# A retention stage ahead of two MLPs: loads behind the decay table, scores of a fifth chunk, and the order of the last rests

## The chip, the core and the metric

The kernel runs on one core of one Trainium2 chip, in one launch. The metric is the device time of an execution in microseconds; the kernel before takes 588.68 us (the median of three runs, 588.51 to 590.65).

## What is computed

Three blocks follow each other, all in float32. First a retention (a linear attention with decay): 2 batches, 8 heads, 768 positions, head size 64. Then an MLP with 512 inputs, 2048 hidden units and a leaky ReLU with a slope per unit, then a second MLP of the same sizes with a squared ReLU. The reference walks over blocks of 64 positions:

```
Dmask = where(i >= j, lam ** (i - j), 0)
intra = ((q_b @ k_b^T) * Dmask) @ v_b
inter = (q_b * lam ** (i + 1)) @ kv_state
out   = intra + inter
kv_state = lam ** block * kv_state + (k_b * lam ** (block - 1 - i))^T @ v_b

x = x @ w_in;  x = max(x, 0) + alpha * min(x, 0);  x = x @ w_out     # first MLP
x = x @ w_in;  x = max(x, 0) ** 2;                 x = x @ w_out     # second MLP
```

The result of the retention, 1536 tokens by 512 channels, is the input of the first MLP.

## The kernel before, in words

**The retention stage.** The kernel uses blocks of 128 positions, so there are 6 steps of 2 batches: 12 chunks, in the order step 0 of both batches, step 1 of both, and so on. Each chunk has four loads of 256 KB: keys `k` and queries `q` (`load_qk`, lines 298 and 299), values `v` and once more the keys, `r`, with positions first (`load_vk`, lines 306 and 310; the last two chunks have no `r`). For chunk n the steps are:

- `scores(n)`: 16 products q k into PSUM (line 422). Only two PSUM buffers exist for them. The scores of chunks 0 and 1 are copied to SBUF by ScalarE (line 427), because the decay table is not there yet; those of later chunks stay in PSUM until the decay.
- `decay(n)`: VectorE multiplies the scores by the decay table `dec` and writes SBUF (line 434).
- `factors(n)`: GpSimd scales `q` by the growth of the decay (line 441, chunks from 2 on) and `r` by the decay to the end of the block (line 444), in place.
- `outputs(n)`: TensorE computes scores times `v` (line 459), `q` times the state (line 467, chunks from 2 on) and the new state product `pk` (line 477).
- `keep_output(n)`: ScalarE rounds the output to the high half of the MLP's input, `xah` (line 486).
- `keep_state(n)`: VectorE adds `pk` to the old state (line 502), ScalarE scales the new one for its next use (line 508, four instructions).
- `keep_rest(n)`: the low half `xal`. For chunks 0 to 8, TensorE subtracts `xah` inside PSUM by a product with a negative unit matrix (`less`, line 495) and ScalarE copies the rest out (line 496). From chunk 9 on (`RESTS`), VectorE subtracts directly (line 493). The PSUM buffer of an output is free only after its rest; there are two, so `outputs(n)` waits for the rest of chunk n-2.

**The decay table.** It holds the powers of lam for all heads. VectorE computes the powers in a chain of small instructions with float32 corrections (lines 347 to 386) into a table `z` of 8 rows; it goes to DRAM (line 391) and comes back spread over 128 partitions as `dec` (line 393, 512 KB). Behind that load, `load_vk(1)` is gated: GpSimd first copies one element of `dec` into `v1` (line 305), so that SP issues no further load until the table has landed. Until then TensorE does the scores of chunks 0 to 3 (`FIRST` = 4), the growth table (line 402) and products with zeros (`keep_warm`, line 320): 12 at the very start and 10 after the scores (`WARM`). Each float32 product shows as two passes.

**Weights.** All MLP products are made in a split form: a float32 number is a rounded high half and a rest, and three products make one. Weights come in 64 pieces of 512 KB (`load_piece`, line 111), three raw buffers, and each is turned into a high and a low tile by a conversion unit: `start` (two ScalarE instructions, lines 122 and 123), `begin` (three VectorE instructions, lines 129 to 131), `middle` (one VectorE instruction, line 139, and ScalarE's rounding, line 141), `end` (one VectorE subtraction, line 150, which waits for the rounding). The first five units are done inside the retention stage, at the chunks marked in `EARLY_UNITS`; eight pieces are loaded at the chunks marked in `EARLY_LOADS`, on SP's queue. A later piece waits for a raw buffer, so for the unit three places before it.

**The order.** The schedule is manual: every engine and queue works through its instructions in program order. The loop over the chunks (lines 522 to 548) issues, for chunk n: the loads `q`, `k` of chunk n+4 and `v`, `r` of chunk n+2, a weight piece if marked; `outputs(n)`; `decay(n+2)`; `begin` of a unit if marked; `keep_output(n)`; `keep_state(n)`; `middle` and `end` of the unit; `start` of the next unit if the next chunk is marked; `factors(n+2)`; `scores(n+3)`; `keep_rest(n)`. After it come the MLPs (lines 561 to 584): 12 products of a hidden tile (line 172), activations, 12 products of the output (lines 225 and 227), with one unit a step.

Of the kernel before, what the change touches and what calls it, by code (L numbers as in the profile page):

```python
# [7 lines left out]
F32 = mybir.dt.float32  # L8
# [8 lines left out]
CH = 128  # L17
NCH = S // CH
NN = B * NCH
NPAIR = H // 2  # L20
# [5 lines left out]
CPT = TT // CH  # L26
ZW = 256
RESTS = 9
FIRST = 4
LA = 3  # L30
DA = 2
AHEAD = 3
# [8 lines left out]
ORDER = [(n // B, n % B) for n in range(NN)]  # L41

LEAST = 2.0**-15
WARM = 12, 10
EARLY_UNITS = [0, 0, 0, 1, 0, 1, 0, 1, 0, 1, 1, 0]
EARLY_LOADS = [0, 1, 1, 0, 1, 0, 1, 0, 1, 1, 1, 1]

SEQ = [0] + [p for f in range(1, 2 * NF) for p in (2 * f, 2 * f - 1)] + [4 * NF - 1]
SEQ[7:9] = SEQ[8:6:-1]
# [4 lines left out]
def retention_then_two_mlps(  # L54
# [15 lines left out]
    nc = tc.nc  # L70
# [83 lines left out]
    conv = Conversion()  # L154
# [114 lines left out]
    actx = ExitStack()  # L269
    ap1 = actx.enter_context(tc.tile_pool(name="ap1", bufs=1))  # L270
    ap2 = actx.enter_context(tc.tile_pool(name="ap2", bufs=2))
    qp = actx.enter_context(tc.tile_pool(name="qp", bufs=LA + 4))
    kp = actx.enter_context(tc.tile_pool(name="kp", bufs=LA + 2))
    scp = actx.enter_context(tc.tile_pool(name="scp", bufs=LA + 1))

    psc = actx.enter_context(tc.tile_pool(name="psc", bufs=2, space=PSUM))
    pso = actx.enter_context(tc.tile_pool(name="pso", bufs=2, space=PSUM))
# [23 lines left out]

    def load_vk(n):
        v_t = kp.tile([128, H, D], F32, tag="v", name=f"v{n}")
        if n == 1:
            nc.gpsimd.tensor_copy(v_t[:, 0, 0:1], dec[:, 0, 0:1])
        nc.sync.dma_start(v_t, vr[n])
        r_t = None
        if ORDER[n][0] < NCH - 1:
            r_t = kp.tile([128, H, D], F32, tag="r", name=f"r{n}")
            nc.sync.dma_start(r_t, kr[n])  # L310
        vk_t[n] = v_t, r_t
# [29 lines left out]
        nc.gpsimd.tensor_copy(head[:, :, t], m)  # L341

    keep_warm(0)
    for n in range(FIRST):
        load_qk(n)

    nc.vector.tensor_copy(sq[:, 0:1], lam_sb)
# [44 lines left out]
    load_vk(0)  # L392
    nc.sync.dma_start(dec, bass.AP(zd[:, :].tensor, zd[:, :].offset, [[1, 128], [ZW, H], [1, CH]]))
    dec_v = dec.rearrange("p (a t) i -> p t a i", t=2)

    grow = ap1.tile([128, NPAIR, CH], F32, name="grow")

# [18 lines left out]
    def scores(n):  # L416
        q_t, k_t = qk_t[n]
        ps = psc.tile([128, 2, NPAIR, CH], F32, tag="s", name=f"s{n}")
        for a in range(NPAIR):
            for t in range(2):  # L420
                rows = slice(t * D, (t + 1) * D)
                nc.tensor.matmul(  # L422
                    ps[:, t, a, :], k_t[rows, a, :], q_t[rows, a, :], start=True, stop=True
                )
        sc = scp.tile([128, 2, NPAIR, CH], F32, tag="sc", name=f"sc{n}")
        if n < FIRST - 2:
            nc.scalar.copy(sc, ps)
            ps = sc
        sc_t[n] = sc, ps

    def decay(n):
        sc, ps = sc_t[n]
        for a in [slice(0, 2), slice(2, 4)] if n == 0 else [slice(0, 4)]:
            nc.vector.tensor_tensor(sc[:, :, a], ps[:, :, a], dec_v[:, :, a], ALU.mult)  # L434

# [14 lines left out]
    def outputs(n):  # L450
        c, b = ORDER[n]
        q_t = qk_t.pop(n)[0]
        v_t, r_t = vk_t.pop(n)
        sc = sc_t.pop(n)[0]
        po = pso.tile([128, NPAIR, CH], F32, tag="o", name=f"o{n}")

        for a in range(NPAIR):
            for t in range(2):
                nc.tensor.matmul(  # L459
                    po[t * D : (t + 1) * D, a, :], v_t[:, 2 * a + t, :], sc[:, t, a, :],  # L460
                    start=a == 0, stop=c == 0, skip_group_check=True,
                )
        if c > 0:
            for a in range(NPAIR):
                for t in range(2):
                    d = slice(t * D, (t + 1) * D)
                    nc.tensor.matmul(  # L467
                        po[d, a, :], state[b, c % 2][d, a, :], q_t[d, a, :], start=False,
                        stop=True, skip_group_check=True,
                    )  # L470
        pk = None
        if c < NCH - 1:
            pk = psk.tile([128, 2, NPAIR, D], F32, tag="pk", name=f"pk{n}")[:, 0]
            for a in range(NPAIR):
                for t in range(2):
                    h = 2 * a + t
                    nc.tensor.matmul(  # L477
                        pk[t * D : (t + 1) * D, a, :], r_t[:, h, :], v_t[:, h, :], start=a == 0,
                        stop=True, skip_group_check=True,
                    )  # L480
        return po, pk
# [28 lines left out]
                )  # L510

    for n in range(FIRST):
        scores(n)
        if n == 2:
            growth()
    keep_warm(1)
    load_vk(1)
    for n in range(2):
        factors(n)
    for n in range(DA):  # L520
        decay(n)
    for n in range(NN):
        if n + FIRST < NN:
            load_qk(n + FIRST)
        if n + 2 < NN:
            load_vk(n + 2)
        if EARLY_LOADS[n]:
# [1 line left out]
        if n == 0:  # L529
            nc.sync.dma_start(alpha_sb, alpha)  # L530
        po, pk = outputs(n)
        if n + DA < NN:
            decay(n + DA)
        if EARLY_UNITS[n]:
            conv.begin()
        keep_output(n, po)
        if pk is not None:
            keep_state(n, pk)
        if EARLY_UNITS[n]:
            conv.middle(load=False)  # L540
            conv.end()
        if n + 1 < NN and EARLY_UNITS[n + 1] or n == NN - 1:
            conv.start(conv.k)
        if n + 2 < NN:
            factors(n + 2)
        if FIRST <= n + LA < NN:
            scores(n + LA)
        keep_rest(n, po)
    actx.close()
    psum["mlp"] = ctx.enter_context(  # L550
        tc.tile_pool(name="psum", bufs=1, space=PSUM, reuse_waits="tile")
# [93 lines left out]
```

## Time and profile before

| | |
|---|---|
| median of three runs | 588.68 us (588.51 to 590.65) |
| the profiled execution | 591.76 us |
| its span | 590.0 us |
| TensorE, products | 578.9 us busy (98%) |
| TensorE, weight loads | 479.9 us (81%) |
| VectorE | 360.1 us (61%) |
| ScalarE | 296.7 us (50%) |
| GpSimd | 28.3 us (5%), all in the first 57 us |

How to read it: the shares are means over the whole span, of which the retention stage is about the first 63 us. Most of the rest is the two MLPs, in which TensorE has no gaps worth a mention. An engine's share over the span therefore says little of the retention stage: GpSimd's 5% are half of its time there. The profiled execution is 3.08 us longer than the median of the unprofiled runs.

### The profile page before, as it was taken

The numbers are of one execution on the slowest core, as the hardware profiler recorded it, in microseconds if no ns is written. First come the engines' busy times: TensorE is split into PE (matmuls) and PEld (weight loads), VectorE is DVE, ScalarE is ACT, GpSimd is POOL, SyncE is SP. The second block draws the span as 40 slices with busy tenths as digits, with TensorE's granted clock in tenths as the row PEclk, the third lists the DMA queues.
The fourth block names the chain that finished last, engine by engine and source line by source line (L and its number), as shares of the span: only waits on it lengthen the run. The fifth ranks groups of instructions, "written<-read, shape, count | busy, mean of one in ns | idle before, by whom it ended". The sixth has DMA issues, their size and how long they took to land.

```text
span 590.0 us, 7970 instructions
## 1 busy us (share of the span) xinstructions
PE 578.9 (98%) x3069; PEld 479.9 (81%) x3069; DVE 360.1 (61%) x616; ACT 296.7 (50%) x515; POOL 28.3 (5%) x31
## 2 busy tenths in 40 slices
PE   8799899999999999999999999999999999999997
PEld 7688788888888888888888888888888888888885
DVE  4489897577578777887887787577522222222422
ACT  2476777566556766576576565555522222321220
POOL 1565000000000000000000000000000000000000
PEclk9799999999999999999999999999999999999999
DMA  6895334332436223233232132332100000400401
GB/s 215 284 390 187 107 112 142 139 108 96 167 130 213 77 103 108 96 118 108 106 111 104 41 139 74 141 107 73 73 0 1 0 1 0 143 0 1 142 1 72
DMA packets 25733, 62.39 MB, mean 106 GB/s; under 512 B 2904, under 2 KB 3936, under 8 KB 25696
## 3 DMA queue, kind: packets, MB, share of 16 engines
q1 hardware_dynamic: 17632, 32.53, 15.7%
q10 hardware_dynamic: 8064, 29.36, 14.5%
q8 instruction: 24, 0.39, 0.3%
q14 instruction: 13, 0.11, 0.1%
HBM read 52.44 MB, written 9.45 MB: 105 GB/s over the span
## 4 chain that ended last, share of the span: by engine, by line
PE 96%; DMA 2%; DVE 1%; issue 0%; DVEq 0%
PE h L172 44%; PE acc L227 22%; PE acc L225 22%; PE o L459 2%; PE o L467 2%; PE s L422 2%; PE pk L477 1%; DMA dec<-zd 1%; PE o L495 1%; DVE sc L434 0%; DMA zd<-z 0%; DMA lam_sb<-in_lam_dram 0%; DVE err L367 0%; DVE sq L349 0%; DVE ps L241 0%
## 5 line engine op out<-in xcount | busy, mean ns | idle before, releaser
L191 ACT CAST gh<-g 128x512 fp32r<-128x512 f32 x96 | 59.7, 621 | 92.6 <-DVE g L182 38.6
L182 DVE SCALAR_TENSOR_TENSOR g<-h,g 128x512 f32<-128x512 f32 x48 | 33.2, 691 | 117.3 <-ACT g L181 117.3
L181 ACT ACTIVATE g<-h 128x512 f32<-128x512 f32 x48 | 28.7, 597 | 124.9 <-PE h L172 124.9
L196 DVE TENSOR_TENSOR gl<-g,gh 128x512 fp32r<-128x512 f32 x96 | 66.5, 692 | 31.0 <-ACT gh L191 22.3
L172 PE MATMUL h<-xah,wl 128*128 128x512 f32 x192 | 74.8, 390 | 0.0
L172 PE MATMUL h<-xah,wh 128*128 128x512 f32 x192 | 74.7, 389 | 0.0
L172 PE MATMUL h<-xal,wh 128*128 128x512 f32 x192 | 74.7, 389 | 0.0
L225 PE MATMUL acc<-gh,wl 128*128 128x512 f32 x192 | 74.7, 389 | 0.0
L225 PE MATMUL acc<-gh,wh 128*128 128x512 f32 x192 | 74.7, 389 | 0.0
L225 PE MATMUL acc<-gl,wh 128*128 128x512 f32 x192 | 74.7, 389 | 0.0
L172 PE MATMUL h<-xbh,wl 128*128 128x512 f32 x192 | 74.7, 389 | 0.0
L172 PE MATMUL h<-xbl,wh 128*128 128x512 f32 x192 | 74.7, 389 | 0.0
L172 PE MATMUL h<-xbh,wh 128*128 128x512 f32 x192 | 74.7, 389 | 0.0
L227 PE MATMUL acc<-wl,gh 128*128 128x512 f32 x192 | 74.7, 389 | 0.0
L227 PE MATMUL acc<-wh,gh 128*128 128x512 f32 x192 | 74.7, 389 | 0.0
L227 PE MATMUL acc<-wh,gl 128*128 128x512 f32 x192 | 74.7, 389 | 0.0
L186 DVE SCALAR_TENSOR_TENSOR g<-h,g 128x512 f32<-128x512 f32 x42 | 29.0, 691 | 41.7 <-ACT g L185 41.6
L150 DVE TENSOR_TENSOR wl<-bits,wh 128x512 fp32r<-128x512 f32 x64 | 44.8, 699 | 3.9 <-ACT wh L141 3.8
L131 DVE SCALAR_TENSOR_TENSOR bits<-raw,bits 128x512 uint32<-128x512 uint32 x64 | 45.1, 704 | 2.2
L139 DVE CUSTOM_DVE_ANT_0 bits<-raw,bits 128x1024 uint16<-128x1024 uint16 x64 | 45.1, 705 | 0.1
L122 ACT ACTIVATE bits<-raw 128x512 f32<-128x512 f32 x64 | 43.1, 674 | 0.0
L123 ACT ACTIVATE raw<-raw 128x512 int32<-128x512 uint32 x64 | 42.8, 669 | 0.0
(81 smaller groups left out, 824.0 us busy)
## 6 DMA issues: line engine op xcount, KB each, us to landing
raw<-in_w_dram ACTq DMA_DIRECT2D x56, 512.0 KB, 3.2
ps<-sums SPq DMA_DIRECT2D x24, 256.0 KB, 3.2
sums<-p SPq DMA_DIRECT2D x20, 256.0 KB, 2.2
raw<-in_w_dram SPq DMA_DIRECT2D x8, 512.0 KB, 6.0
k<-in_kt_dram SPq DMA_DIRECT2D x12, 256.0 KB, 5.7
q<-in_qt_dram SPq DMA_DIRECT2D x12, 256.0 KB, 5.4
v<-in_vr_dram SPq DMA_DIRECT2D x12, 256.0 KB, 6.0
r<-in_kr_dram SPq DMA_DIRECT2D x10, 256.0 KB, 5.3
```

Of the source, the lines that this page charges most:

```text
L122: nc.scalar.activation(x.bitcast(F32), high.bitcast(F32), AF.Abs)
L123: nc.scalar.activation(low.bitcast(I32), low, AF.Copy, scale=2.0**-29)
L131: nc.vector.scalar_tensor_tensor(x, high, 0xC0000000, x, ALU.bitwise_and, ALU.bitwise_or)
L139: nc.vector.tensor_tensor(x.bitcast(I32), x.bitcast(I32), low.bitcast(I32), ALU.add)
L150: nc.vector.tensor_tensor(lo, x, hi.bitcast(F32), ALU.subtract)
L172: nc.tensor.matmul(ph, w[:, cols], x[:, c, :], start=c == 0 and i == 0, stop=c == NC - 1 and i == 2)
L182: nc.vector.scalar_tensor_tensor(g, ph, 0.0, g, ALU.max, ALU.mult)
L186: nc.vector.scalar_tensor_tensor(g, ph, 0.0, g, ALU.max, ALU.subtract)
L191: nc.scalar.copy(gh, g)
L196: nc.vector.tensor_tensor(gl, g, gh.bitcast(F32), ALU.subtract)
L225: nc.tensor.matmul(acc[t][i], w[:, cols], g, **flags)
L227: nc.tensor.matmul(acc[t][i], g[:, cols], w, **flags)
```

## The change

Six things are edited. The scores of five chunks instead of four are computed ahead of the loop, and those of chunks 0 to 3 are copied to SBUF, so their decays run in place. The zero products stand ahead of the fifth chunk's scores, and are 12 instead of 10. The gate on `v1` is gone, and `q4`, `k4`, `v1`, `r1`, `q5`, `k5` are loaded right behind the table; in the loop the loads of `q` and `k` run six chunks ahead instead of four, with more buffers. The early units stand at chunks 3, 5, 6, 8, 9 instead of 3, 5, 7, 9, 10, and some pieces are loaded at other chunks. For chunks 9 to 11 the rest (line 493 of the kernel before) stands ahead of `middle` and `end` of a unit. For chunks 0 and 2, which have no scores behind them any more, the rest is issued after the next chunk's outputs.

```diff
@@ -26,7 +26,7 @@
 CPT = TT // CH
 ZW = 256
 RESTS = 9
-FIRST = 4
+FIRST = 5
 LA = 3
 DA = 2
 AHEAD = 3
@@ -41,9 +41,9 @@
 ORDER = [(n // B, n % B) for n in range(NN)]
 
 LEAST = 2.0**-15
-WARM = 12, 10
-EARLY_UNITS = [0, 0, 0, 1, 0, 1, 0, 1, 0, 1, 1, 0]
-EARLY_LOADS = [0, 1, 1, 0, 1, 0, 1, 0, 1, 1, 1, 1]
+WARM = 12, 12
+EARLY_UNITS = [0, 0, 0, 1, 0, 1, 1, 0, 1, 1, 0, 0]
+EARLY_LOADS = [0, 1, 1, 0, 1, 1, 0, 1, 1, 1, 1, 0]
 
 SEQ = [0] + [p for f in range(1, 2 * NF) for p in (2 * f, 2 * f - 1)] + [4 * NF - 1]
 SEQ[7:9] = SEQ[8:6:-1]
@@ -269,9 +269,9 @@
     actx = ExitStack()
     ap1 = actx.enter_context(tc.tile_pool(name="ap1", bufs=1))
     ap2 = actx.enter_context(tc.tile_pool(name="ap2", bufs=2))
-    qp = actx.enter_context(tc.tile_pool(name="qp", bufs=LA + 4))
-    kp = actx.enter_context(tc.tile_pool(name="kp", bufs=LA + 2))
-    scp = actx.enter_context(tc.tile_pool(name="scp", bufs=LA + 1))
+    qp = actx.enter_context(tc.tile_pool(name="qp", bufs=FIRST + 4))
+    kp = actx.enter_context(tc.tile_pool(name="kp", bufs=FIRST + 1))
+    scp = actx.enter_context(tc.tile_pool(name="scp", bufs=FIRST))
 
     psc = actx.enter_context(tc.tile_pool(name="psc", bufs=2, space=PSUM))
     pso = actx.enter_context(tc.tile_pool(name="pso", bufs=2, space=PSUM))
@@ -301,8 +301,6 @@
 
     def load_vk(n):
         v_t = kp.tile([128, H, D], F32, tag="v", name=f"v{n}")
-        if n == 1:
-            nc.gpsimd.tensor_copy(v_t[:, 0, 0:1], dec[:, 0, 0:1])
         nc.sync.dma_start(v_t, vr[n])
         r_t = None
         if ORDER[n][0] < NCH - 1:
@@ -341,7 +339,7 @@
         nc.gpsimd.tensor_copy(head[:, :, t], m)
 
     keep_warm(0)
-    for n in range(FIRST):
+    for n in range(FIRST - 1):
         load_qk(n)
 
     nc.vector.tensor_copy(sq[:, 0:1], lam_sb)
@@ -392,6 +390,9 @@
     load_vk(0)
     nc.sync.dma_start(dec, bass.AP(zd[:, :].tensor, zd[:, :].offset, [[1, 128], [ZW, H], [1, CH]]))
     dec_v = dec.rearrange("p (a t) i -> p t a i", t=2)
+    load_qk(FIRST - 1)
+    load_vk(1)
+    load_qk(FIRST)
 
     grow = ap1.tile([128, NPAIR, CH], F32, name="grow")
 
@@ -422,14 +423,17 @@
                 nc.tensor.matmul(
                     ps[:, t, a, :], k_t[rows, a, :], q_t[rows, a, :], start=True, stop=True
                 )
-        sc = scp.tile([128, 2, NPAIR, CH], F32, tag="sc", name=f"sc{n}")
-        if n < FIRST - 2:
+        if n < FIRST - 1:
+            sc = scp.tile([128, 2, NPAIR, CH], F32, tag="sc", name=f"sc{n}")
             nc.scalar.copy(sc, ps)
             ps = sc
-        sc_t[n] = sc, ps
+        sc_t[n] = ps
 
     def decay(n):
-        sc, ps = sc_t[n]
+        ps = sc = sc_t[n]
+        if n >= FIRST - 1:
+            sc = scp.tile([128, 2, NPAIR, CH], F32, tag="sc", name=f"sc{n}")
+        sc_t[n] = sc
         for a in [slice(0, 2), slice(2, 4)] if n == 0 else [slice(0, 4)]:
             nc.vector.tensor_tensor(sc[:, :, a], ps[:, :, a], dec_v[:, :, a], ALU.mult)
 
@@ -451,7 +455,7 @@
         c, b = ORDER[n]
         q_t = qk_t.pop(n)[0]
         v_t, r_t = vk_t.pop(n)
-        sc = sc_t.pop(n)[0]
+        sc = sc_t.pop(n)
         po = pso.tile([128, NPAIR, CH], F32, tag="o", name=f"o{n}")
 
         for a in range(NPAIR):
@@ -510,18 +514,19 @@
                 )
 
     for n in range(FIRST):
+        if n == FIRST - 1:
+            keep_warm(1)
         scores(n)
         if n == 2:
             growth()
-    keep_warm(1)
-    load_vk(1)
     for n in range(2):
         factors(n)
     for n in range(DA):
         decay(n)
+    pending = []
     for n in range(NN):
-        if n + FIRST < NN:
-            load_qk(n + FIRST)
+        if n + FIRST + 1 < NN:
+            load_qk(n + FIRST + 1)
         if n + 2 < NN:
             load_vk(n + 2)
         if EARLY_LOADS[n]:
@@ -529,23 +534,33 @@
         if n == 0:
             nc.sync.dma_start(alpha_sb, alpha)
         po, pk = outputs(n)
+        for x in pending:
+            keep_rest(*x)
+        pending = []
         if n + DA < NN:
             decay(n + DA)
-        if EARLY_UNITS[n]:
+        if EARLY_UNITS[n] and n < NN - 2:
             conv.begin()
         keep_output(n, po)
         if pk is not None:
             keep_state(n, pk)
+        if n >= RESTS:
+            keep_rest(n, po)
         if EARLY_UNITS[n]:
+            if n >= NN - 2:
+                conv.begin()
             conv.middle(load=False)
             conv.end()
         if n + 1 < NN and EARLY_UNITS[n + 1] or n == NN - 1:
             conv.start(conv.k)
         if n + 2 < NN:
             factors(n + 2)
-        if FIRST <= n + LA < NN:
-            scores(n + LA)
-        keep_rest(n, po)
+        ahead = FIRST if n == 1 else n + LA
+        if n == 1 or FIRST < ahead < NN:
+            scores(ahead)
+            keep_rest(n, po)
+        elif n < RESTS:
+            pending = [(n, po)]
     actx.close()
     psum["mlp"] = ctx.enter_context(
         tc.tile_pool(name="psum", bufs=1, space=PSUM, reuse_waits="tile")
```

## Rows read from the trace of the kernel before

**Rows 1.** The chain of waits, first 66 us: start us, length us, what ran.

```profile
9.75 6.44 DMA dec<-zd
...
18.50 1.12 PE o L459 x8
...
21.19 1.91 PE o L459 x16
...
23.10 0.85 PE pk L477 x16
...
23.95 1.44 PE s L422 x16
...
26.85 1.02 PE o L467 x16
...
27.87 0.62 PE pk L477 x16
...
28.49 1.09 PE s L422 x16
...
29.58 0.42 PE o L495
...
59.72 1.73 issue
...
63.56 2.49 PE h L172 x10
```

**Rows 2.** Timeline of TensorE before the table lands; SP's queue waits.

```profile
12.35 2.50 PE L320 MATMUL warm_ps<-warm 128*128 128x128 f32 x20
...
17.03 0.66 PE L459 MATMUL o<-sc,v 128*64 128x128 f32 x8 [2.18 <-DVE sc L434]
...
SPq L306 <- POOL v L305: 6.2, 1, 6.2
```

**Rows 3.** By stretch: length, PE, PEld, DVE, ACT, POOL, clock, DMA share, GB/s.

```profile
10.00:15.00 5.00, 4.85 (x49) 4.29 (x46) 0.69 (x1) 0.00 (x0) 0.00 (x0) 1.00 0.68 187
...
14.50:15.00 0.50, 0.35 (x4) 0.16 (x2) 0.00 (x0) 0.00 (x0) 0.00 (x0) 1.00 0.01 1
...
17.50:18.00 0.50, 0.19 (x4) 0.00 (x0) 0.50 (x1) 0.00 (x0) 0.40 (x1) 0.83 0.75 164
...
30.00:35.00 5.00, 5.00 (x82) 4.19 (x81) 4.73 (x6) 3.58 (x10) 2.84 (x2) 1.00 1.04 390
...
30.70:60.70 30.00, 28.99 (x461) 23.54 (x456) 25.39 (x35) 19.64 (x48) 17.53 (x13) 1.00 0.74 270
```

**Rows 4.** Timeline, VectorE beside GpSimd: start, length, engine, line.

```profile
31.68 1.43 DVE L131 SCALAR_TENSOR_TENSOR bits<-raw,bits 128x512 uint32<-128x512 uint32 x1
...
37.99 1.22 DVE L434 TENSOR_TENSOR sc<-s,dec 128x1024 f32<-128x1024 f32 x1 [0.35 <-PE s L422]
...
38.29 1.06 POOL L444 TENSOR_TENSOR r<-r,dec 128x512 f32<-128x512 f32 x1
...
51.52 1.43 DVE L139 CUSTOM_DVE_ANT_0 bits<-raw,bits 128x1024 uint16<-128x1024 uint16 x1
...
54.79 1.29 POOL L441 TENSOR_TENSOR q<-q,grow 128x512 f32<-128x512 f32 x1 [2.38 <-PE s L422]
```

**Rows 5.** Timeline of VectorE, unit of chunk 9 and the rest behind it.

```profile
56.84 0.41 DVE L129 TENSOR_SCALAR bits<-bits 128x512 f32<-128x512 f32 x1
...
57.75 0.69 DVE L131 SCALAR_TENSOR_TENSOR bits<-raw,bits 128x512 uint32<-128x512 uint32 x1
...
58.36 0.42 DVE L502 TENSOR_TENSOR state<-pk,old 128x256 f32<-128x256 f32 x1
...
58.69 0.68 DVE L139 CUSTOM_DVE_ANT_0 bits<-raw,bits 128x1024 uint16<-128x1024 uint16 x1
...
60.06 0.69 DVE L150 TENSOR_TENSOR wl<-bits,wh 128x512 fp32r<-128x512 f32 x1 [0.68 <-ACT wh L141]
...
60.67 0.68 DVE L493 TENSOR_TENSOR xal<-o,xah 128x512 fp32r<-128x512 f32 x1
```

## The prediction

> **What bounds the kernel now.** I read the chain of waits over the first 66 us first, because the page says that TensorE is busy for 98% of the span: whatever the change does, it does before the two MLPs. The chain [rows 1] shows three things. The decay table's load holds everything until 16.19. From 18.50 the chain is TensorE alone, chunk after chunk. And there is one hole, 1.73 us at 59.72, just ahead of outputs(11). The first MLP matmul follows at about 63.5, and from there to the last sum TensorE has no gap that this change touches. So the question is only when that matmul starts: a microsecond there is a microsecond of the whole.
>
> Next I read the start of the retention stage [rows 2]. The zero products run from 12.35, TensorE then idles 2.18 us, does half of outputs(0) at 17.03 and waits again until 18.50. The granted clock is full at 14.5 to 15.0 and falls to one half between 17.5 and 18.0 [rows 3]; the first outputs cost 1.91 and 0.85 us where later ones cost 1.02 and 0.62, and scores(4) 1.44 where scores(5) cost 1.09 [rows 1].
>
> Last I read who makes the hole at 59.72. outputs(11) writes the PSUM buffer that the rest of chunk 9 reads. That rest is the subtraction at line 493, and VectorE reaches it at 60.67 [rows 5]. It waits for nothing but VectorE itself: from 30.7 to 60.7 VectorE is busy 25.39 of 30 us [rows 3], and what is left are mostly pauses inside a conversion unit, where it waits for ScalarE's rounding. VectorE is thus the second bound of this stage, nearly level with TensorE. Part of its time is lost to GpSimd. Line 131 takes 0.69 us when GpSimd is done, but 1.43 at 31.68, beside a GpSimd scaling; there are six such instructions up to 51.52, 4.92 us more than their undisturbed lengths in all, over the units of chunks 3, 5 and 7, or 1.64 a unit [rows 4, 5]. The unit of chunk 9 loses nothing, since GpSimd's last scaling, begun at 54.79, is over by 56.08 [rows 4]. A decay read from PSUM loses nothing either (1.22 us at 37.99, beside a scaling) [rows 4].
>
> **The change, part by part.** The sum is made against the profiled execution (591.76 us, span 590.0); its shift is then applied to the median of the runs, 588.68, which lies 3.08 us lower.
>
> Scores(4) ahead of the table. The loads k4 and q4 now stand right behind the table on SP's queue, without the gate that held v1's load back for 6.2 us [rows 2]. The table's bytes are out by 14.5, when the DMA engines are nearly still [rows 3]. Two loads of 256 KB at the 390 GB/s of a full stretch [rows 3] take 1.34 us: 15.84 at the earliest. The table itself landed 1.7 us after its last bytes, so 17.5 at the latest likely; I take 17.5, since the same slow tail lies ahead of them. Scores(4) then ends at 18.6 and outputs(0), queued behind it on TensorE, starts there, 0.1 us after the second half could have begun. Every further microsecond of landing would cost one.
>
> Twelve zero products for ten. 20 passes took 2.50 us [rows 2], so 24 take 3.00: from 12.35 to 15.35. TensorE then idles until 17.5, about as long as now. Whether the clock falls is open, so I carry both.
>
> Two more score copies on ScalarE: it is idle in that stretch, 0.00 us busy from 10 to 15 [rows 3]; they cost nothing. Decays 2 and 3 now read SBUF and can collide with GpSimd. They are needed only after outputs(1), so the first cover is TensorE's own work; with that gone each would cost a scaling, 1.06 us [rows 4].
>
> TensorE's lead at chunk 2. Full clock: outputs(0) and its state product from 18.6, 1.02 + 0.62, until 20.2. GpSimd's scaling for chunk 1 now finds its data early and stands in front of decay(1): 18.45 + 1.06 + 1.22 = 20.7. outputs(1) with its state product until 22.4; two rests of 0.42 and scores(5) of 1.09 until 24.3; outputs(2) with 1.02 + 1.02 + 0.62 until 27.0 (all from [rows 1]). Now that product ends at 28.49, so the lead is 1.5. At half clock the first two outputs and products cost 1.91 + 0.85 each instead of 1.64: 2.24 more, 0.7 late. The middle of the two is a lead of **0.4**.
>
> Loads, SP. Query and key loads run two chunks further ahead; SP issues them sooner, and the weight pieces keep their waits for a free raw buffer. v11 stands behind the piece of chunk 8, which waits for the unit of chunk 6; it is hidden while that unit is done some 4 us before outputs(11).
>
> Units and rests. Chunks 3, 5, 7, 9, 10 become 3, 5, 6, 8, 9. Now four whole units stand ahead of the rest of chunk 9. Afterwards there are again four (3, 5, 6, 8), and the first three instructions of the fifth as well, because its begin stays ahead of the rest and only its second half moves behind. These three cost 58.36 - 56.84 = **1.52 us** [rows 5]. The gain meant by the reordering, the second half of a unit moved behind the rest, is spent by having started a further unit.
>
> Collisions. The last query scaling cannot run before scores(11), which TensorE does in chunk 8, so GpSimd now works beside all four units: at 1.64 a unit, 1.64 more. Two pairs of units (5, 6 and 8, 9) have no plain chunk between them in which scalings could pass beside a PSUM decay. Lower bound: nothing more than now. Upper bound: every scaling of the four unit chunks costs VectorE its whole length, (1.06 + 1.29) x 4 - 4.92 = 4.5 [rows 4]. I take **2.2**, the middle, near the 1.64 that rows give.
>
> Sum at line 493 of chunk 9: -0.4 + 1.52 + 2.2 = 3.3 us later, 60.67 becomes 64.0. What follows it (outputs(11), then the MLP) is unchanged, so 588.68 + 3.3 = **592.0 us**.
>
> The Trainium skill speaks against this part of the change: its page "SBUF — State Buffer" (section "SBUF: two separate sides") says that VectorE and GpSimd share one pair of ports as an exclusive lock, held for a whole instruction, with the loser fully blocked, also for a VectorE instruction with two SBUF inputs. The 1.43 us at 31.68 against 0.69 agrees. By that rule alone the collision term is the upper bound and the sum about 594.3; by the average that these rows show it is near 592.
>
> **Rivals.** (1) *VectorE finds room, and TensorE sets the pace.* From 27.0: outputs(3) 2.66, two rests and scores 1.93, five chunks of 2.66 + 1.09 + 0.42, outputs(9) 2.66 and outputs(10) 2.04 end at 57.1, where outputs(11) starts at 61.45 now: 4.3 us sooner, **584.4**. For it: the earlier loads, and a rest that no longer waits for a unit's second half. Against it: VectorE would have to reach that rest by 56.4, with 1.52 us more in front of it; nearly all its collisions would have to vanish. It decides from the point at which line 493 starts before 60.67. Chance 0.15.
>
> (2) *The terms nearly cancel.* Full clock with its lead of 1.5, and collisions between now's and 1.64 more: 0.0 to 1.7 late, **589.5** in the middle. For it: GpSimd, fed sooner, may finish scalings in VectorE's pauses. Against it: the doubled units. Chance 0.33.
>
> (3) *The table comes late.* Six loads, 1.5 MB, run behind it with no gate; at 390 GB/s they are 4 us of traffic, and if a third of that lands ahead of the table's tail it is 1.3 us more on top: **593.3**. Against it: they are issued after the table, on the same queue. Chance 0.10.
>
> That the change does not do what it says is inside the first term: the zeros end at 15.35, about 0.8 us ahead of the table.
>
> **How the numbers follow.** The forecast, VectorE late by about 3 us, has 0.42; with (3), slower by over 0.5% (2.94 us, about what a measurement of this kernel can tell from no change) gets 0.52. (2) gives 0.33 within 0.5%. (1) gives 0.15 faster. The upper end is half clock with all collisions, 0.7 + 1.52 + 4.5 = 6.7: 595.4. The lower end leaves out most of (1): 586.0. Cases of both signs hold most of the chance; the likeliest one's own range is 590.4 to 595.4.
>
> **What would show it.** Right: line 493 of chunk 9 starts at 62 or later and outputs(11) waits longer than 1.73 us; TensorE shows waits also ahead of outputs(7) to (10); VectorE's unit instructions of chunks 5, 6 and 8 show lengths of 1.2 to 1.6. The lead at chunk 2 is seen in the end of the third state product, 27.0 or 29.2 against 28.49, and in the clock at 18 to 24. Wrong: line 493 before 60, with TensorE unbroken from outputs(2) to the MLP; then (1) holds. If the table lands after 17, (3) does.

## The result and the profile after

The changed kernel takes 593.13 us (median of 8 runs, 590.71 to 594.74), the kernel before beside it 588.61 us (8 runs, 588.14 to 590.65): a ratio of 1.0069, interval 1.0047 to 1.0091 (a ratio, here and below, is estimated from all runs of both kernels and isn't the quotient of the medians). On another chip the same two kernels gave 1.0044 (experiment 8). So the change costs 0.4 to 0.7%; 592.0 us was forecast. The profiled execution took 594.73 us, its span 592.7 us, against 591.76 and 590.0 before. The two profiled executions are thus 3.0 us apart, the medians 4.5: the profiled one of before is slower than all eight of its runs, so what follows accounts for the 2.7 us between two spans, not for the whole loss.

The chain of waits of the changed kernel (start us, length us, what ran), to lay beside [rows 1]:

```profile
10.40 7.88 DMA q<-in_qt_dram
...
18.41 1.16 PE s L423 x16
...
26.55 0.64 PE pk L481 x16
...
38.80 1.43 DVE bits L131
...
42.60 1.54 DVE wl L150
...
49.98 0.62 ACT wh L141
50.60 0.48 ACT xal L500
51.09 0.50 ACT xah L490
...
51.63 0.80 PE o L499
52.42 1.91 PE o L463 x16
54.33 1.90 PE o L471 x16
...
63.74 0.60 issue
...
66.46 1.59 PE h L172 x6
```

Before, the chain was TensorE alone from 18.50 to one hole at 59.72. Now it is TensorE up to the third state product, which ends at 27.19 and not at 28.49, so 1.3 us were won early against this profile. From there to 51.6 it runs to and fro between VectorE and ScalarE. The hole ahead of outputs(11) has shrunk from 1.73 to 0.60 us, and yet the first MLP product comes at 66.46 instead of 63.56, 2.9 us late.

TensorE's timeline shows where it waits now (in brackets: idle time before, and what ended it):

```profile
18.41 1.16 PE L423 MATMUL s<-q,k 64*128 64x128 f32 x16 [3.34 <-DMA q<-in_qt_dram]
...
44.72 0.51 PE L499 MATMUL o<-xah,less 128*128 128x512 f32 x1 [0.83 <-ACT xah L490]
...
51.63 0.80 PE L499 MATMUL o<-xah,less 128*128 128x512 f32 x1 [2.65 <-ACT xah L490]
...
64.34 1.09 PE L463 MATMUL o<-sc,v 128*64 128x128 f32 x16 [0.63 <-PE o L471]
```

The product with `less` (L499) needs `xah`, which ScalarE writes in program order behind the scaling of the last state (L512) and the rounding `wh` of a unit (L141). Both wait for VectorE: the first for its state sum (line 506), which stands behind the unit's begin, the second for its line 139. ScalarE's timeline has the longer wait at the state sum:

```profile
48.91 1.06 ACT L512 ACTIVATE old<-state,grow 128x64 f32<-128x64 f32 x4 [4.25 <-DVE state L506]
```

A late unit so reaches TensorE through ScalarE. The stretches (columns as in [rows 3]) show what the wait of 2.65 us brings with it:

```profile
14.50:15.00 0.50, 0.50 (x6) 0.38 (x4) 0.00 (x0) 0.00 (x0) 0.00 (x0) 1.00 1.05 348
...
17.50:18.00 0.50, 0.00 (x0) 0.00 (x0) 0.50 (x2) 0.00 (x0) 0.50 (x1) 1.00 1.01 381
...
20.00:25.00 5.00, 4.93 (x88) 4.17 (x86) 5.00 (x4) 4.02 (x13) 4.68 (x3) 1.00 0.96 309
...
30.70:60.70 30.00, 26.45 (x362) 21.25 (x360) 24.52 (x30) 18.26 (x45) 17.46 (x13) 0.89 0.67 246
...
50.00:55.00 5.00, 3.37 (x25) 2.61 (x27) 3.76 (x5) 3.39 (x9) 1.07 (x1) 0.62 0.48 162
55.00:60.00 5.00, 5.00 (x61) 4.12 (x57) 3.37 (x6) 3.04 (x6) 1.18 (x1) 0.70 0.13 28
```

The granted clock was full at 20 to 25 us, where before it was 0.53. It falls to 0.62 and 0.70 at 50 to 60 instead, and outputs(8) costs 1.91 and 1.90 us where 1.02 each is usual. Between 30.7 and 60.7 TensorE has lost 2.5 us of busy time (26.45 for 28.99).

VectorE's timeline, the lines that answer to [rows 4, 5], and the GpSimd scalings beside them:

```profile
17.01 7.50 DVE L438 TENSOR_TENSOR sc<-sc,dec 128x512 f32<-128x512 f32 x5 [5.18 <-DMA dec<-zd]
...
29.40 0.43 DVE L129 TENSOR_SCALAR bits<-bits 128x512 f32<-128x512 f32 x1 [0.56 <-ACT bits L122]
...
33.05 1.60 DVE L150 TENSOR_TENSOR wl<-bits,wh 128x512 fp32r<-128x512 f32 x1 [1.10 <-ACT wh L141]
...
38.80 1.43 DVE L131 SCALAR_TENSOR_TENSOR bits<-raw,bits 128x512 uint32<-128x512 uint32 x1
...
42.60 1.54 DVE L150 TENSOR_TENSOR wl<-bits,wh 128x512 fp32r<-128x512 f32 x1 [0.68 <-ACT wh L141]
...
46.85 1.64 DVE L131 SCALAR_TENSOR_TENSOR bits<-raw,bits 128x512 uint32<-128x512 uint32 x1
...
57.32 0.42 DVE L506 TENSOR_TENSOR state<-pk,old 128x256 f32<-128x256 f32 x1 [0.88 <-PE pk L481]
...
59.03 1.62 DVE L150 TENSOR_TENSOR wl<-bits,wh 128x512 fp32r<-128x512 f32 x1 [0.69 <-ACT wh L141]
...
61.71 0.41 DVE L129 TENSOR_SCALAR bits<-bits 128x512 f32<-128x512 f32 x1
...
63.56 0.68 DVE L497 TENSOR_TENSOR xal<-o,xah 128x512 fp32r<-128x512 f32 x1
```

```profile
42.54 1.06 POOL L448 TENSOR_TENSOR r<-r,dec 128x512 f32<-128x512 f32 x1 [1.16 <-DMA r<-in_kr_dram]
43.55 1.74 POOL L445 TENSOR_TENSOR q<-q,grow 128x512 f32<-128x512 f32 x1
45.25 1.28 POOL L448 TENSOR_TENSOR r<-r,dec 128x512 f32<-128x512 f32 x1
46.49 1.44 POOL L445 TENSOR_TENSOR q<-q,grow 128x512 f32<-128x512 f32 x1
47.90 1.50 POOL L448 TENSOR_TENSOR r<-r,dec 128x512 f32<-128x512 f32 x1
49.37 1.71 POOL L445 TENSOR_TENSOR q<-q,grow 128x512 f32<-128x512 f32 x1
...
58.82 1.28 POOL L445 TENSOR_TENSOR q<-q,grow 128x512 f32<-128x512 f32 x1 [7.74 <-PE s L423]
```

Nine unit instructions ahead of the rest of chunk 9 are drawn out, 6.70 us over their undisturbed lengths (0.42, 0.43, 0.69, 0.68 and 0.69 us for lines 129, 130, 131, 139 and 150), against six and 4.92 us before. The worst stretch is 38.8 to 51.6 us, the units of chunks 5 and 6, over which GpSimd scales with few pauses: 4.86 of the 6.70 us are lost there. The rest (L497, line 493 before) starts at 63.56 instead of 60.67. The 2.89 us between them add up: the unit of chunk 3 starts 1.37 us earlier (29.40 for 30.77); the begin of the fifth unit now stands in front (61.71 to 63.22, 1.51); 1.78 more of drawn-out lengths; and some 0.9 that VectorE waits for a state product which TensorE does at half clock (the 0.88 at 57.32). -1.37 + 1.51 + 1.78 + 0.9 = 2.8. The decays of chunks 0 to 3, which now all read SBUF, take 7.50 us in five instructions from 17.01, but TensorE shows no wait worth a line between 18.41 and 44.72, so they hold it up nowhere.

### The profile page after: what moved, and what is told of

Its sections match the earlier page's. It is cut to its first block, busy times and chain, and to the rows that moved or that the text cites. A ratio compares the mean times of both kernels' runs of the same rounds, so it can differ in the third digit from the quotient of the medians.

```text
span 592.7 us, 7966 instructions
## 1 busy us (share of the span) xinstructions
PE 580.1 (98%) x3073; PEld 481.0 (81%) x3073; DVE 363.9 (61%) x616; ACT 298.5 (50%) x517; POOL 30.1 (5%) x30
## 4 chain that ended last, share of the span: by engine, by line
PE 92%; DVE 4%; DMA 2%; ACT 2%; issue 0%; SPq 0%; ACTq 0%; DVEq 0%
PE h L172 44%; PE acc L227 22%; PE acc L225 22%; DMA q<-in_qt_dram 1%; PE o L463 1%; PE o L471 1%; ACT old L512 1%; DVE bits L131 1%; PE pk L481 1%; DVE wl L150 1%; PE s L423 0%; DVE sc L438 0%; PE o L499 0%; DVE bits L130 0%; ACT wh L141 0%
## 5 line engine op out<-in xcount | busy, mean ns | idle before, releaser
L225 PE MATMUL acc<-gh,wh 128*128 128x512 f32 x192 | 74.7, 389 | 0.0
L225 PE MATMUL acc<-gh,wl 128*128 128x512 f32 x192 | 74.7, 389 | 0.0
L225 PE MATMUL acc<-gl,wh 128*128 128x512 f32 x192 | 74.7, 389 | 0.0
L186 DVE SCALAR_TENSOR_TENSOR g<-h,g 128x512 f32<-128x512 f32 x42 | 29.0, 691 | 42.9 <-ACT g L185 42.8
L150 DVE TENSOR_TENSOR wl<-bits,wh 128x512 fp32r<-128x512 f32 x64 | 46.9, 732 | 3.9 <-ACT wh L141 3.8
```

Of the source, the lines that this page charges most:

```text
L150: nc.vector.tensor_tensor(lo, x, hi.bitcast(F32), ALU.subtract)
L186: nc.vector.scalar_tensor_tensor(g, ph, 0.0, g, ALU.max, ALU.subtract)
L225: nc.tensor.matmul(acc[t][i], w[:, cols], g, **flags)
```

## The experiments

The theory at the outset: VectorE sets the MLP's start, by the units ahead of the last rests and by the time they lose beside GpSimd; the early part (loads, five scores, zeros) helps a little. The rival: the early part, or the order of the last rests, is where the time goes. Each comparison below rests on 12 runs against 35 of the kernel before on the same chip: one chip for experiments 1 to 4, another for 5 to 8, a third for 9 to 12. The changed kernel itself ran on the second of these alone.

### 1. The changed kernel with the units of before

```diff
-EARLY_UNITS = [0, 0, 0, 1, 0, 1, 1, 0, 1, 1, 0, 0]
-EARLY_LOADS = [0, 1, 1, 0, 1, 1, 0, 1, 1, 1, 1, 0]
+EARLY_UNITS = [0, 0, 0, 1, 0, 1, 0, 1, 0, 1, 1, 0]
+EARLY_LOADS = [0, 1, 1, 0, 1, 0, 1, 0, 1, 1, 1, 1]
```

> The changed kernel, with the units and weight pieces back at the chunks of before (3, 5, 7, 9, 10). Theory V (VectorE sets the end of the stage): ahead of the rest of chunk 9 stand three whole units and the first three instructions of a fourth, one whole unit less than in the changed kernel; that unit is 2.9 us of VectorE work and up to 1.7 us of collisions, so the rest starts 3 to 5 us earlier, near 59.5, and the time is 588 to 590.5. Theory T (the loss comes from the early part: table 0.8 us late, fifth scores ahead of it): the time stays at 592 to 593.

Measured: 590.02 us, ratio 0.9999 [0.9981, 1.0017]. The whole loss hangs on where the units and their weight pieces stand (the two were moved together in every experiment that moves units). Everything else in the change is together worth nothing measurable, though it moves the rest of chunk 9 to 56.26, 4.4 us earlier than in the kernel before. VectorE's and TensorE's timelines tell where that went:

```profile
56.26 0.68 DVE L497 TENSOR_TENSOR xal<-o,xah 128x512 fp32r<-128x512 f32 x1
...
67.42 0.69 DVE L186 SCALAR_TENSOR_TENSOR g<-h,g 128x512 f32<-128x512 f32 x1 [1.16 <-ACT g L185]
...
68.82 0.50 PE L225 MATMUL acc<-gh,wl 128*128 128x512 f32 x1 [1.15 <-ACT gh L191]
```

The MLP starts at 59.2, but its first activations queue behind the fifth unit and the last rests on VectorE and ScalarE, and TensorE waits 1.15 us there.

### 2. Begin of chunk 9 behind the rest

```diff
-        if EARLY_UNITS[n] and n < NN - 2:
+        if EARLY_UNITS[n] and n < RESTS:
             conv.begin()
...
-            if n >= NN - 2:
+            if n >= RESTS:
                 conv.begin()
```

> The changed kernel, with one edit: for chunk 9 the first three VectorE instructions of its unit also stand behind the rest. Theory V: these cost 61.71 to 63.22, 1.5 us, so the rest starts near 62.0 and the time falls by 1.5 us to about 591.6. Theory T: no difference, 593.

Measured: 591.95 us, 1.0034 [1.0017, 1.0051]. Without the begin in front of the rest 0.34% of loss stays, where the changed kernel has 0.44 and 0.69% on other chips. What is gone is compatible with the 1.5 us of the begin, and the larger part stays by the first of these figures, about half by the second; experiment 10 shows more clearly that the begin is not the main part. The unit of chunk 6 still holds up TensorE as in the changed kernel (TensorE's timeline):

```profile
50.18 0.80 PE L499 MATMUL o<-xah,less 128*128 128x512 f32 x1 [2.65 <-ACT xah L490]
```

### 3. The kernel before, with only the last rests moved

```diff
-        if EARLY_UNITS[n]:
+        if EARLY_UNITS[n] and n < RESTS:
             conv.begin()
...
+        if n >= RESTS:
+            keep_rest(n, po)
         if EARLY_UNITS[n]:
+            if n >= RESTS:
+                conv.begin()
...
-        keep_rest(n, po)
+        if n < RESTS:
+            keep_rest(n, po)
```

> The kernel before, with only the rests of chunks 9 to 11 ahead of the whole units of those chunks. Theory V: the rest of chunk 9 no longer stands behind a unit (56.84 to 60.67 in the trace of before, less the state's 0.4), so it is ready before TensorE wants it at 59.7; the hole of 1.73 us goes and the time is 587.0. Rival: the order of the rest is without effect because the hole has another cause, 588.6.

Measured: 591.48 us, 1.0024 [1.0005, 1.0043]: a miss. (The profiled execution, 593.27 us, is the slowest of the twelve.) The hole of [rows 1] ahead of outputs(11) is gone, and a larger one has opened at 73 (VectorE's and TensorE's timelines):

```profile
58.86 0.68 DVE L493 TENSOR_TENSOR xal<-o,xah 128x512 fp32r<-128x512 f32 x1
...
71.67 0.69 DVE L186 SCALAR_TENSOR_TENSOR g<-h,g 128x512 f32<-128x512 f32 x1 [1.16 <-ACT g L185]
...
73.07 0.50 PE L225 MATMUL acc<-gh,wl 128*128 128x512 f32 x1 [2.27 <-ACT gh L191]
```

Two units, three rests and a begin still stand in front of the first activation (L186). Putting a rest ahead of a unit does not shorten the queue; it moves the wait from the rest to the activation. The step "the gain meant by the reordering" in the prediction took for granted that there was one.

### 4. The changed kernel's early part alone

The units as in experiment 1, and the order of begin and rests as in the kernel before.

```diff
-        if EARLY_UNITS[n] and n < NN - 2:
+        if EARLY_UNITS[n]:
             conv.begin()
...
-        if n >= RESTS:
-            keep_rest(n, po)
...
-            if n >= NN - 2:
-                conv.begin()
...
+        else:
+            keep_rest(n, po)
```

> The changed kernel's early part alone (loads behind the table with no gate, five scores ahead, zeros, two rests after the next outputs), with units and last rests where they were before. Theory V: the lead of 1.3 us at chunk 2 reaches the rest of chunk 9 through VectorE, less up to 1 us of new collisions: 587.3 to 588.6. Theory T: the early part is the loss, 591 or more.

Measured: 589.74 us, 1.0000 [0.9982, 1.0019]. That part of the theory falls: in this order of the rests the early part gives nothing back. The hole before outputs(11) is there again (TensorE's timeline), since VectorE's units set its end and not TensorE's lead:

```profile
60.02 1.09 PE L463 MATMUL o<-sc,v 128*64 128x128 f32 x16 [1.25 <-issue]
```

Whether the early part helps with the rests in front stays open: experiment 1, which has both, is 1.5 us below experiment 3 on the same chip, but experiment 5 is 0.9 us above 7 (in both pairs the begin of chunk 9 stands elsewhere as well).

### 5 and 7. One early unit less

Five is the changed kernel, seven is the kernel of experiment 3, both with four units, at chunks 3, 5, 7 and 9; the fifth is left to the MLP's steps. The new lines:

```diff
+EARLY_UNITS = [0, 0, 0, 1, 0, 1, 0, 1, 0, 1, 0, 0]
+EARLY_LOADS = [0, 1, 1, 0, 1, 0, 1, 0, 1, 1, 1, 0]
```

> The changed kernel with four units ahead of the MLPs instead of five, at chunks 3, 5, 7 and 9, and seven pieces loaded instead of eight. Theory V2 (VectorE's whole backlog at the start of the MLPs is the bound, whatever its order): one unit less there, so neither a hole ahead of outputs(11) nor the wait of 1.15 us at 66 to 69 that the run with units at 3, 5, 7, 9, 10 showed; 1 to 2 us below the kernel before, ratio 0.997 to 0.998. Rival: the unit left out is missed a few steps later, the MLP waits for its weights, and the time is at or above the kernel before.

> The kernel before with its early part untouched, four units at chunks 3, 5, 7, 9 and the last rests ahead of the units. Theory V2: the wait at 70 to 75 that the run with the rests alone showed (2.3 us) goes, and so does the hole of 1.73 us: 1 to 2 us below the kernel before. If it equals the run with the changed early part, that part is worth nothing; if it is 1 to 1.5 us slower than it, the early part's lead counts as soon as VectorE is relieved.

Measured: 588.78 us, 0.9980 [0.9963, 0.9996], and 587.85 us, 0.9972 [0.9954, 0.9990]. Both beat both kernels, and the one without the early part is at least as good. VectorE is nearly clear when the MLP begins. The hole of 2.27 us that experiment 3 has ahead of the first L225 is gone in seven; behind it there is another wait, for a weight tile (TensorE's timeline):

```profile
70.75 0.50 PE L172 MATMUL h<-xah,wl 128*128 128x512 f32 x1 [0.51 <-DVE wl L150]
```

### 6. The changed kernel without most scalings

The scaling of the queries by the growth is left out for chunks 5 to 11, and that of the keys by the decay to the end of the block for chunks 5 to 9, so that GpSimd is idle beside most units.

```diff
+        if n >= 5:
+            return
         c = ORDER[n][0]
```

> The changed kernel without GpSimd's scalings for chunks 5 to 11: the queries of these chunks are not scaled by the growth of the decay and their keys not by the decay to the block's end, so only the load on GpSimd differs. Theory V with the collision term: in the changed kernel nine unit instructions lose 6.7 us to GpSimd; without them VectorE reaches the rest of chunk 9 near 58, the first MLP product follows near 60 to 61 and the time is 4 to 6 us below the changed kernel, at or below the kernel before. Rival: VectorE is late by its own work (units too close together, a begin ahead of the rest), and the collisions cost 1 us or less in the end.

Measured: 586.42 us, 0.9950 [0.9933, 0.9967], 5.96 us below the changed kernel on the same chip (experiment 8). In the profile the rest of chunk 9 starts 5.59 us earlier than at 63.56, and the drawn-out lengths ahead of it fall from 6.70 to 0.88 us (VectorE's timeline):

```profile
57.97 0.68 DVE L499 TENSOR_TENSOR xal<-o,xah 128x512 fp32r<-128x512 f32 x1
```

So the time that units lose beside GpSimd is worth what it measures. How much of it the change added isn't shown by this: the kernel before loses 4.92 us in its profile too, and it was not run without its scalings.

### 8. The changed kernel again

No edit; it stands beside 5, 6 and 7.

> The changed kernel once more, beside the three others on one chip. Both theories: 4 to 4.5 us above the kernel before, ratio 1.007; it is the reference for the leave-out run.

Measured: 592.38 us (590.14 to 596.06), 1.0044 [1.0024, 1.0064], less than the 1.007 expected. In its profile the drawn-out lengths are 4.72 us instead of 6.70, the rest starts at 61.73 instead of 63.56, and the span is 590.8 instead of 592.7. The two profiles of the changed kernel thus differ by about as much as their units are drawn out; that its other executions differ for the same reason is likely, but not shown.

### 9. Seven, with the units a chunk earlier

```diff
+EARLY_UNITS = [0, 0, 1, 0, 1, 0, 1, 0, 1, 0, 0, 0]
+EARLY_LOADS = [1, 1, 0, 1, 0, 1, 0, 1, 1, 1, 0, 0]
```

> The four-unit version on the old start (ratio 0.997 to the kernel before, its small hole in TensorE at 70 to 75 us) with the units a chunk earlier: chunks 2, 4, 6, 8 for 3, 5, 7, 9, and their loads a chunk earlier too. If the place of the last unit matters beside the amount of VectorE's work, VectorE is clear when the MLP's first activations come, the hole (about 0.5 us) goes, and the ratio is about 0.996. If the amount alone counts, the ratio stays at 0.997. If the unit at chunk 2 or the earlier piece loads stand in the way of the first decays, TensorE waits at 20 to 30 us and the ratio is 0.999 or more.

Measured: 589.59 us, 0.9998 [0.9980, 1.0016]: the gain of seven is gone. TensorE waits 0.51 us ahead of 30.64 for a query load. It waits 0.78 us ahead of 45.13; the profile puts this down to a query load as well, though ScalarE's `xah`, which that product reads, ends only at 45.07. The drawn-out lengths are 6.12 us, the most of any spread units. Whether the earlier weight pieces hold up the query load, and which of the two costs the gain, isn't shown.

### 10 and 11. Four whole units ahead of the last rest, close together and spread

Ten is the changed kernel without its fifth unit, so with units at 3, 5, 6, 8; eleven is the kernel before without its fifth, with units at 3, 5, 7, 9 and its own order of rests.

```diff
+EARLY_UNITS = [0, 0, 0, 1, 0, 1, 1, 0, 1, 0, 0, 0]
+EARLY_LOADS = [0, 1, 1, 0, 1, 1, 0, 1, 1, 1, 0, 0]
```

```diff
+EARLY_UNITS = [0, 0, 0, 1, 0, 1, 0, 1, 0, 1, 0, 0]
+EARLY_LOADS = [0, 1, 1, 0, 1, 0, 1, 0, 1, 1, 1, 0]
```

> The changed kernel with its fifth unit left to the MLP: units at chunks 3, 5, 6, 8 and seven loads, so two of the four still stand in neighbouring chunks. If the number of units ahead of the MLP decides, it is like the four spread units on the new start: ratio 0.998 to the kernel before. If it is the neighbouring units (5, 6) and their collisions with GpSimd, most of the changed kernel's loss stays: 1.002 to 1.005, with TensorE waits at 44 and 51 us as in the changed kernel.

> The kernel before with one early unit less (chunks 3, 5, 7, 9; seven loads) and nothing else, so the second half of the unit of chunk 9 still stands ahead of the last rest and the hole at 59.72 can stay. If VectorE's amount of work is the bound, it gains most of what four units with the rests ahead gained: 0.997 to 0.998. If the order of the rest is worth something by itself once a unit is gone, it gains little: 0.999 to 1.000, with the hole of 1 to 1.7 us ahead of outputs(11) kept.

Measured: ten 593.12 us, 1.0048 [1.0027, 1.0068]; eleven 590.12 us, 1.0000 [0.9981, 1.0019]. In both, four whole units stand ahead of the rest of chunk 9, and ten is 3.0 us slower. The early part, another difference between them, is worth nothing as far as experiment 4 shows. So the loss comes from units in neighbouring chunks, not from their number. The weight pieces moved with the units, by a chunk; in neither profile does VectorE, ScalarE or TensorE wait for a piece ahead of the MLP, but a piece can also shift the loads that GpSimd's scalings wait for, and that isn't separated here. VectorE's timeline of ten, the unit of chunk 6 and the rest:

```profile
46.32 0.88 DVE L129 TENSOR_SCALAR bits<-bits 128x512 f32<-128x512 f32 x1
47.23 1.16 DVE L130 TENSOR_SCALAR bits<-bits 128x512 uint32<-128x512 uint32 x1
...
51.16 1.61 DVE L150 TENSOR_TENSOR wl<-bits,wh 128x512 fp32r<-128x512 f32 x1 [1.10 <-ACT wh L141]
...
62.24 0.68 DVE L497 TENSOR_TENSOR xal<-o,xah 128x512 fp32r<-128x512 f32 x1
```

and of eleven, the unit of chunk 7 and the rests of chunks 9 and 10 in one row:

```profile
46.58 1.38 DVE L130 TENSOR_SCALAR bits<-bits 128x512 uint32<-128x512 uint32 x1
...
50.72 1.59 DVE L150 TENSOR_TENSOR wl<-bits,wh 128x512 fp32r<-128x512 f32 x1 [1.10 <-ACT wh L141]
...
58.66 1.28 DVE L493 TENSOR_TENSOR xal<-o,xah 128x512 fp32r<-128x512 f32 x2
```

In eleven five instructions are drawn out, 2.29 us in all, three of them by more than 0.2 us; ten has ten such instructions, 6.88 us in all, nine of them by more than 0.2. Eleven also shows that one unit less is no gain by itself: it keeps a hole of 1.38 us ahead of outputs(11) at 59.44. The gain of seven needs both edits, the rest in front (which alone costs 0.24%) and a unit less behind it (which alone gives nothing).

### 12. Seven again

No edit; beside 9, 10 and 11.

> The four-unit version on the old start, unchanged, beside the other three on this chip: 0.997 to the kernel before, as on the chip before. A ratio of 0.999 or more would mean that the gain is within what chips differ by.

Measured: 588.54 us, 0.9966 [0.9946, 0.9986].

### All profiles in one table

Of each profile: the whole units ahead of the rest of chunk 9, the time by which their instructions are drawn out (differences under 0.03 us left out), the start of that rest, the one less the other, the first MLP product's start in TensorE's timeline, how far it lies behind the rest, and the span less it. "Close" means that two of the units stand in neighbouring chunks, "a begin" that the first three instructions of one more unit stand ahead of the rest.

| kernel | units ahead | drawn out | rest | rest less drawn out | MLP | MLP less rest | span less MLP |
|---|---|---|---|---|---|---|---|
| before | 4 | 4.92 | 60.67 | 55.75 | 63.49 | 2.82 | 526.5 |
| 4 | 4 | 3.44 | 59.23 | 55.79 | 62.06 | 2.83 | 526.3 |
| 11 | 4 | 2.29 | 58.66 | 56.37 | 61.49 | 2.83 | 526.9 |
| 10 | 4, close | 6.88 | 62.24 | 55.36 | 65.07 | 2.83 | 526.9 |
| after | 4, close, a begin | 6.70 | 63.56 | 56.86 | 66.39 | 2.83 | 526.3 |
| 8 | 4, close, a begin | 4.72 | 61.73 | 57.01 | 64.55 | 2.82 | 526.3 |
| 6 | 4, close, a begin | 0.88 | 57.97 | 57.09 | 60.80 | 2.83 | 526.3 |
| 9 | 4, a chunk earlier | 6.12 | 58.23 | 52.11 | 61.05 | 2.82 | 527.0 |
| 2 | 4, close | 5.77 | 59.33 | 53.56 | 62.81 | 3.48 | 526.3 |
| 1 | 3, a begin | 4.71 | 56.26 | 51.55 | 59.22 | 2.96 | 528.0 |
| 5 | 3, a begin | 5.16 | 57.25 | 52.09 | 60.19 | 2.94 | 526.9 |
| 3 | 3 | 4.39 | 58.86 | 54.47 | 62.35 | 3.49 | 529.2 |
| 7 | 3 | 3.83 | 55.58 | 51.75 | 59.06 | 3.48 | 527.0 |
| 12 | 3 | 4.45 | 57.05 | 52.60 | 60.53 | 3.48 | 527.1 |

Where the MLP follows by 2.82 or 2.83 us, VectorE's rest sets its start, and nothing else varies between rest and MLP. There the rest comes at the length of the work ahead of it (55.4 to 56.4 with four units, 56.9 to 57.1 with a begin more, and 52.1 in 9, whose units all stand a chunk earlier) plus the drawn-out time. In the other six the rest is early enough and TensorE goes its own pace to the MLP; in 2 that pace is set by waits as in the changed kernel. The last column is what is paid later: 2.7 us in 3 over the 526.5 of before, where VectorE's queue was only reordered, 1.5 in 1, and 0.5 in 7.

## Why the prediction was right, and where it was not

**The bound** was right: between the two profiles the time is the start of the first MLP matmul plus a constant (526.5 and 526.3 us), and VectorE's way to line 493 of chunk 9 sets that start. The forecast had line 493 at 64.0; it came at 63.56. That a microsecond at this start is always one of the whole is not so: in experiments 1 and 3, 1.5 and 2.7 us of it are paid later.

**The landing of `q4`** was put at 17.5 and came at 18.28. The table itself landed at 17.0, 0.8 us later than before, with loads moving 348 GB/s at 14.5 to 15.0 where 1 went before, and 381 at 17.5 to 18.0 for 164. That looks like rival 3, but it isn't shown: the other profile of the changed kernel (experiment 8) has the first decay at 16.09, and over all profiles it starts at 15.21 to 17.01 with the loads behind the table (eight) and at 14.81 to 16.29 without (six). And the early part as a whole, the table's landing included, costs nothing measurable (experiments 1 and 4).

**The lead at chunk 2** was taken as 0.4, the middle of 1.5 (full clock) and -0.7 (half). It was 1.3 in this profile, at full clock; in experiment 8, the same kernel, the clock was 0.86 and 0.80 over the ten microseconds from 15 on and the lead 0.6. What failed is that the lead was measured against one execution of the kernel before. Its third state product, which ends at 28.49, is the latest of the six profiles with the old start (25.89 to 28.49, four of them below 26.9); the eight with the new start have 25.59 to 27.99. So no lead is left that the early part could be said to give, and experiment 4 gains nothing measurable: 0.5 us ahead of the profile of before at that product, it has its rest, less the drawn-out time, at 55.79 where that of before has 55.75.

**The begin of the fifth unit** was priced at 1.52 and took 1.51. The table agrees: 1.2 us between the means of the two arrangements, 55.8 and 57.0. But experiment 10, which takes away the whole unit, leaves most or all of the loss (1.0048), and experiment 2, which takes away the begin, half or more of it, so it isn't the main reason. It decides less than the sum gave it: with it gone, TensorE meets its own waits (experiment 2), or a unit more in the MLP (experiment 10, 526.9 for 526.3 in the last column).

**The collisions** were priced at 2.2 and added 1.78 in the profile of after. Of the reasons given, the units with no plain chunk between them are borne out: leaving the scalings out gives 5.96 us back, and the close units cost 3.0 us against spread ones. But of the two pairs only the first lost more: units 5 and 6 are drawn out by 4.86 us, where 5 and 7 were by 3.43, while unit 8 lost 0.93 and the begin of 9 nothing. What the term missed is its spread: the drawn-out time is 4.72 to 6.70 us in two profiles of one kernel, and 2.29 to 4.92 in the three profiles with four units at 3, 5, 7 and 9 ahead of the rest, so that one profile's rows say little of the median. With 4.92, the profile of before had the highest of these three, and the sum took it as the kernel's own: a reason, not shown, why the medians moved by 4.5 us and not by 3.3. The exclusive lock between VectorE and GpSimd of which the Trainium skill tells ("SBUF — State Buffer", section "SBUF: two separate sides") agrees with 1.64 us at 46.85 for 0.69. By that rule alone the term was put at 4.5; the trace has 1.78, and 17.5 us of GpSimd work between 30.7 and 60.7 (the stretch above) drew units out by only 6.70.

**A term was missing:** the way from a late unit through ScalarE's order (`wh`, then `xah`) to TensorE, and back as a late state product at half clock, 0.9 us. The prediction expected TensorE waits ahead of outputs(7) to (10), and they came (0.83 and 2.65 us, at the products with `less` behind outputs(6) and outputs(7)), but it gave them no price. The errors of the sum nearly cancel: 0.9 more was won early, 0.4 less was lost to collisions, and 0.9 was lost to this wait. That the forecast came so near to line 493 is in part luck.

**One sign was wrong:** outputs(11) was to wait longer than 1.73 us. It waited 0.60, as TensorE was by then late by itself.

**The rivals.** (1) fell: TensorE was broken at 44.7, 51.6 and 63.7, and line 493 started after 60.67. (3) is answered above. (2), the terms nearly cancel, is not far off on the second chip, where the interval of 1.0024 to 1.0064 reaches down to a quarter of a per cent. What stays open is why the medians before differ between the chips (588.61 over 8 runs, 589.83 to 590.26 over 35); nothing here was tried on that.

What was not tried: three early units, since the MLP's steps then come to a piece before its unit is made, and a scaling of keys on ScalarE instead of GpSimd, which would test a cure and not only the cost. Nor were units moved without their weight pieces, or the kernel before run without its scalings.

## What to carry to other kernels

When a wait ends behind a queue of one engine's work, putting the awaited instruction forward pays only if the work that it overtakes is not awaited next; look one stage further before counting the gain. Spread work that loses time beside another engine over stretches in which that engine is idle or the work is of another kind: here four units of which two stood in neighbouring chunks cost about 3 us more than four with a chunk between each two. Take a price from several executions where they differ by as much as the price: here a lead of 1.3 us against one profile of before was none against four of the five others with the same start. And test two edits together as well as one by one, as here neither of the two gained alone and both gained 0.3%.

## What the hardware showed unexpectedly

The length of TensorE's idle time alone did not tell whether the granted clock would fall: in the profile after it stayed at 1.00 over a wait of 3.34 us at 15 to 18.4 and fell to 0.62 after one of 2.65 us at 51.6. Among the other starts, 2.76 us (experiment 5) and 2.90 us (experiment 1) left it full, while it was 0.92 and 0.74 over the two stretches of five microseconds from 15 on after 2.94 us (experiment 4), and 0.86 and 0.80 after 1.96 us (experiment 10). The same kernel's executions differ by up to 6 us (590.14 to 596.06 in experiment 8), where leaving most scalings out brought 10 of 12 runs within 1.5 us (585.85 to 587.35); the other two lay at 589.06 and 590.53. Experiment 5, with all its scalings, has its twelve runs within 2.9 us, so the scalings alone don't make the spread.
